# A constant tile multiplied six times a slot in the first batch, and values loaded from SyncE's queue in three portions

## The chip, the cores and the metric

The kernel runs on one core of a Trainium2 chip. A core has TensorE (PE, matmuls; its weight loads are listed apart as PEld), VectorE (DVE), ScalarE (ACT), GpSimd (POOL) and SyncE (SP, which here only issues DMAs). DMAs are issued from SyncE's queue (SPq) or ScalarE's queue (ACTq). The metric is the device time of one execution in microseconds, as the median of the runs.

## The reference

Attention with rotated queries and keys over 4 batches of 8 heads, 576 positions and 64 channels, and then two pairs of dense layers over the 2304 tokens, all in float32:

```python
q_rot, k_rot = (rotate(q), rotate(k))
scores = (1.0 / np.sqrt(D)) * np.matmul(q_rot, k_rot.transpose(0, 1, 3, 2))
scores = scores - np.max(scores, axis=-1, keepdims=True)
attn = np.exp(scores)
attn = attn / (np.sum(attn, axis=-1, keepdims=True) + 1e-09)
x = np.matmul(attn, v)                  # -> x: 2304 tokens of 512 channels
h = x @ w_in;  r = np.maximum(h, 0.0);  x = (s * (r * r) + b) @ w_out
h = x @ w_in2; x = (h / (1.0 + np.exp(-1.702 * h))) @ w_out2
```

## The kernel before, in words

**Slots.** The program is laid out in slots, numbered from below zero up. `at(slot, fn, ...)` puts a task in a slot, and within a slot the table `ORDER` sorts the tasks. Attention takes 144 slots, 36 a batch. A batch has 4 pairs of heads, a pair has two units of 4 and 5 tiles of 128 queries, and each tile is one slot. The tasks of slot n for a tile are: `score_tile` (TensorE writes the scores s of 128 queries against 576 keys into two PSUM banks, of which there is one pair; VectorE reads them into P with the row's minimum, L422; ScalarE takes the exponent, L431), two slots later `turn_tile` (five transposes of P into the PSUM tile t, whose high part ScalarE copies into pt, L491, and whose remainder VectorE takes in every third slot, L497), one slot after that `rest_tile` in the other slots (two matmuls with the constant tile `minus`, then ScalarE, L514), and at the end of a unit `spread_sums` (small matmuls of the row sums with `minus`) and `weighted` (30 matmuls av with the values). TensorE's instructions are chained with `pin` and run in the order in which the code writes them; the other engines' orders come from a scheduler.

**The start.** Before slot 0, `plan_rope` loads the keys and queries of the first pairs (`rope_load`, L257, SyncE's queue), rotates the first pair's on VectorE and the others' on GpSimd (L266 to L274), transposes them on TensorE into r (`rope_turn`, L283), splits r into z (ScalarE's cast of the high part, L295; VectorE's remainder, L296) and places z with DMAs as the operands k and qa of the scores (`place_k`, L321 and L322, four DMAs; `place_qa`, L331 to L333, twelve). A pair's rotated tile is turned in two groups, of 128 and of 64 rows, through a single PSUM bank.

**The values.** `value_load` brings a pair's values with five DMAs (L373 and L378). In the first batch all four pairs are loaded in slot -5, twenty DMAs from ScalarE's queue. `v_top` (slot 1), `v_first` (slot 2) and `v_spread` (slot 3) take the largest magnitude of each head and make its scale, `value_split` (slot 4 for the first pair) splits the values into two float16 parts vz.

**The weights.** In the first batch `weight` loads and converts the first 8 of 16 blocks of the first dense layer pair, in 16 halves: a DMA of 512 KB into a stage tile, then on VectorE L572, L573, L576 and L581 and on ScalarE L571 and L579. These stand from slot 2 on, and the scheduler puts them where it finds room. The dense layers themselves start a few slots after the first batch and then run between the attention of the later batches, by a fixed plan of slots.

## Time and profile before

| what | us |
|---|---|
| median of 3 runs (1296.07 to 1302.21) | 1296.47 |
| the profiled execution's own time | 1298.34 |
| its span, first to last instruction | 1296.6 |
| TensorE busy in the span | 1127.2 |
| VectorE busy | 729.9 |
| ScalarE busy | 676.6 |
| mean granted TensorE clock, share of full | 0.959 |

Times within the profile are microseconds from the span's start. The views used below are: busy time of each engine by stretch ("windows"), instructions in order of time ("timeline", where an entry in brackets is the idle time of the engine just before and what ended it), groups of instructions by line and shape, and DMA issues by line.

### The profile page before, as it was taken

The numbers are of one execution on the slowest core, as the hardware profiler recorded it, in microseconds if no ns is written. First come the engines' busy times: TensorE is split into PE (matmuls) and PEld (weight loads), VectorE is DVE, ScalarE is ACT, GpSimd is POOL, SyncE is SP. The second block draws the span as 40 slices with busy tenths as digits, with TensorE's granted clock in tenths as the row PEclk, the third lists the DMA queues.
The fourth block names the chain that finished last, engine by engine and source line by source line (L and its number), as shares of the span: only waits on it lengthen the run. The fifth ranks groups of instructions, "written<-read, shape, count | busy, mean of one in ns | idle before, by whom it ended". The sixth has DMA issues, their size and how long they took to land.

```text
span 1296.6 us, 20786 instructions
## 1 busy us (share of the span) xinstructions
PE 1127.2 (87%) x7520; PEld 998.5 (77%) x7520; DVE 729.9 (56%) x1653; ACT 676.6 (52%) x1489; POOL 280.4 (22%) x292
## 2 busy tenths in 40 slices
PE   0346777789789899998999999988999999999998
PEld 0235555689689899998999889876888888888887
DVE  5895456879567765666656483667533223232222
ACT  1356665767567666666666575566433223232232
POOL 7631403115414432441111020323000000000000
PEclk9968887899899999999999989999999999999999
DMA  7774576788768776667653384445203012020020
GB/s 205 193 227 101 113 173 208 235 262 260 235 198 238 239 241 179 204 176 213 193 169 120 122 294 132 150 159 177 100 27 104 1 49 82 17 82 16 25 73 17
DMA packets 139398, 194.74 MB, mean 150 GB/s; under 512 B 31648, under 2 KB 103840, under 8 KB 139296
## 3 DMA queue, kind: packets, MB, share of 16 engines
q1 hardware_dynamic: 134368, 192.23, 49.5%
q10 hardware_dynamic: 4928, 1.18, 0.5%
q8 instruction: 60, 0.98, 0.3%
q14 instruction: 42, 0.34, 0.1%
HBM read 145.65 MB, written 40.63 MB: 144 GB/s over the span
## 4 chain that ended last, share of the span: by engine, by line
PE 57%; DMA 10%; issue 8%; DVE 8%; ACT 4%; POOL 1%; SPq 0%; DVEq 0%; ACTq 0%; POOLq 0%
PE acc L99 23%; PE l L99 22%; PE s L99 4%; PE av L99 4%; PE t L99 4%; DMA stage<-in_moe_w_in_dram 3%; DMA stages<-in_moe_w_in_dram 2%; DVE pt L495 1%; DVE P L422 1%; ACT pt L491 1%; DMA qb<-qsp 1%; POOL w L581 1%; ACT P L431 1%; DMA stage<-in_moe_w_out_dram 1%; DMA ksp<-z 1%
## 5 line engine op out<-in xcount | busy, mean ns | idle before, releaser
L99 PE MATMUL l<-xh,w 128*128 128x256 f32 (+1 forms) x1280 | 330.8, 332 | 7.6 <-DVE r L710 4.8
L99 PEld LDWEIGHTS l<-xh,w 128*128 128x128 f32 x1280 | 224.5, 191 | 31.5 <-DVE r L710 8.3
L99 PE MATMUL l<-xl,w 128*128 128x256 f32 (+1 forms) x640 | 211.1, 330 | 0.0
L99 PE MATMUL acc<-w,g 128*128 128x512 f32 x696 | 168.9, 392 | 3.4 <-ACT y L755 3.4
L714 DVE SCALAR_TENSOR_TENSOR r<-r,l 128x256 f32<-128x256 f32 x144 | 60.1, 417 | 180.3 <-ACT r L713 180.3
L442 POOL TENSOR_SCALAR P<-P,st 128x576 f32<-128x576 f32 x108 | 87.7, 812 | 314.8 <-DVE st L441 216.6
L99 PEld LDWEIGHTS acc<-w,g 128*128 128x128 f32 x696 | 131.5, 189 | 31.3 <-ACT y L755 3.8
L431 ACT ACTIVATE P<-P,st 128x576 f32<-128x576 f32 x144 | 111.7, 776 | 75.2 <-DVE P L422 74.7
L713 ACT ACTIVATE r<-l 128x256 f32<-128x256 f32 x144 | 55.1, 382 | 179.0 <-PE l L99 179.0
L422 DVE TENSOR_SCALAR_CACHE_REDUCE P<-s 128x576 f32<-128x576 f32 x144 | 108.5, 754 | 68.0 <-PE s L99 67.1
L99 PEld LDWEIGHTS l<-xl,w 128*128 128x128 f32 x640 | 122.0, 191 | 11.2
L99 PE MATMUL acc<-gh,w 128*128 128x256 f32 x616 | 128.2, 291 | 0.0
L99 PE MATMUL t<-ident,P 128*128 128x128 f32 x720 | 110.1, 287 | 20.7 <-DVE pt L495 9.0
L718 DVE TENSOR_TENSOR g<-r,g 128x256 fp32r<-128x256 f32 x160 | 74.1, 463 | 67.2 <-ACT g L717 67.2
L711 ACT ACTIVATE r<-r,sb 128x256 f32<-128x256 f32 x144 | 86.4, 600 | 49.0 <-DVE r L710 48.8
L491 ACT ACTIVATE pt<-t 128x640 f16<-128x640 f32 x144 | 100.7, 699 | 16.9 <-PE t L99 16.7
L99 PEld LDWEIGHTS t<-ident,P 128*128 128x128 f32 x720 | 86.3, 148 | 28.4 <-issue 19.6
L495 DVE TENSOR_TENSOR pt<-t,pt 128x640 f16<-128x640 f32 x108 | 88.6, 821 | 27.7 <-ACT pt L491 27.4
L99 PEld LDWEIGHTS acc<-gh,w 128*128 128x128 f32 x616 | 103.0, 194 | 0.7 <-DVE part L753 0.2
L717 ACT CAST g<-r 128x256 fp32r<-128x256 f32 x160 | 64.9, 406 | 64.0 <-DVE r L714 63.7
L99 PE MATMUL l<-xh,ws 128*128 128x256 f32 (+1 forms) x384 | 89.4, 311 | 5.3 <-DMA ws<-wd 2.8
L99 PE MATMUL s<-k,qb 128*128 128x320 f32 x480 | 88.1, 311 | 5.0 <-DVE P L422 3.3
(133 smaller groups left out, 2006.4 us busy)
## 6 DMA issues: line engine op xcount, KB each, us to landing
ws<-wd SPq DMA_DIRECT2D x96, 512.0 KB, 4.4
k<-ksp SPq DMA_DIRECT2D x24, 576.0 KB, 5.4
stage<-in_moe_w_in_dram SPq DMA_DIRECT2D x25, 512.0 KB, 4.9
stage<-in_moe_w_out_dram SPq DMA_DIRECT2D x25, 512.0 KB, 4.2
wd<-w SPq DMA_DIRECT2D x14, 512.0 KB, 4.1
xl<-xT SPq DMA_DIRECT2D x11, 512.0 KB, 5.8
xl<-x SPq DMA_DIRECT2D x9, 512.0 KB, 4.3
out_dram<-y SPq DMA_DIRECT2D x36, 128.0 KB, 2.4
```

What stands on the lines that cost most here:

```text
L99: pin(nc.tensor.matmul(*args, **kw))
L422: nc.vector.tensor_scalar(pr, ps[:, 192 : 192 + S], -Q_SCALE, None, op0=ALU.mult, op1=ALU.min, accum_out=st[:, 0:1],)
L431: nc.scalar.activation(pr, pr, AF.Exp, bias=st[:, 0:1], scale=-1.0, accum_out=total)
L442: nc.gpsimd.tensor_scalar(pr, pr, st[:, 2:3], 1.0, op0=ALU.mult, op1=ALU.mult)
L491: nc.scalar.activation(hi, pc, AF.Copy, scale=1.0 if u["b"] else P_SCALE)
L495: nc.vector.tensor_tensor(lo, pc, hi, op=ALU.subtract)
L581: eng.tensor_tensor(lo, f32(low), f32(hi), op=ALU.subtract)
L711: nc.scalar.activation(r, r, AF.Identity, bias=sb[:, 1:2], scale=sb[:, 0:1])
L713: nc.scalar.activation(r, ps[:, cols], AF.Tanh, scale=0.851)
L714: nc.vector.scalar_tensor_tensor(r, r, 1.0, ps[:, cols], op0=ALU.add, op1=ALU.mult)
L717: nc.scalar.copy(gh[:, cols], r)
L718: nc.vector.tensor_tensor(gl[:, cols], r, f32(gh[:, cols]), op=ALU.subtract)
```

## The change

`keep_busy` is new. It multiplies `minus` (128x128, bfloat16) by itself, read twice as 256 columns, and writes columns 768 to 1023 of the current score tile, which nothing reads; it does so three times a call. It is called after the scores of each tile of the first batch, and after each `turn_tile` that falls into a slot of the first batch: 36 and 34 calls, 210 matmuls. `value_load` uses SyncE's queue in the first batch too, in slots -5, -5, -2 and -1 for the four pairs. `v_top`, `v_first`, `v_spread` and the first `value_split` move one slot later.

```diff
+    FILL = 3
+    spare = {}
+    def keep_busy():
+        for _ in range(FILL):
+            mm(spare["s"][:, 768:1024], minus,
+               minus.unsqueeze(1).to_broadcast([128, 2, 128]),
+               start=True, stop=True, skip_group_check=True)
...
-        queue = nc.sync if b else nc.scalar
-        ins = queue.dma_start(vr[64:128, :, 4], vs[:, :, 8])
+        ins = nc.sync.dma_start(vr[64:128, :, 4], vs[:, :, 8])
...
     def score_tile(u):
...
+        if u["b"] == 0:
+            spare["s"] = ps
+            keep_busy()
...
     def turn_tile(u):
...
+        if u["n"] + SKEW_T < bounds[1]:
+            keep_busy()
...
-                at(-5, value_load, b, p, vts[p])
-                at(1, v_top, b, p, vts, first_scale)
-                at(first - 2 if p else 4, value_split, b, p, vts[p])
+                at((-5, -5, -2, -1)[p], value_load, b, p, vts[p])
+                at(2, v_top, b, p, vts, first_scale)
+                at(first - 2 if p else 5, value_split, b, p, vts[p])
...
-    at(2, v_first, 0, first_scale)
-    at(3, v_spread, 0, first_scale)
+    at(3, v_first, 0, first_scale)
+    at(4, v_spread, 0, first_scale)
```

SyncE's queue from its fourth DMA on, before (naturals, nat and values are areas that hold keys and queries as loaded, stage the weights, k00 the first pair's placed keys):

```order
L257 DMA naturals_103<-in_k_dram 128x576 x2
L257 DMA naturals_103<-in_q_dram 128x576 x2
L257 DMA naturals_103<-in_k_dram 128x576
L257 DMA nat020_242<-in_q_dram 128x576
L562 DMA stage0_00_245<-in_moe_w_in_dram 128x4x128
L567 DMA stage0_01_342<-in_moe_w_out_dram 128x512
L562 DMA stage0_10_424<-in_moe_w_in_dram 128x4x128
L567 DMA stage0_11_506<-in_moe_w_out_dram 128x512
L257 DMA nat031_564<-in_k_dram 128x576
L257 DMA values_132<-in_q_dram 128x576
L322 DMA k00_167<-z001_155 64x4x128 x2
```

The same place now (vr00 and vr01 are the first two pairs' values):

```order
L257 DMA naturals_103<-in_k_dram 128x576 x2
L257 DMA naturals_103<-in_q_dram 128x576 x2
L372 DMA vr00_118<-in_v_dram 64x2x64
L372 DMA vr01_125<-in_v_dram 64x2x64
L377 DMA vr00_118<-in_v_dram 64x4x64
L377 DMA vr01_125<-in_v_dram 64x4x64 x2
L377 DMA vr00_118<-in_v_dram 64x4x64
L377 DMA vr01_125<-in_v_dram 64x4x64
L377 DMA vr00_118<-in_v_dram 64x4x64 x2
L377 DMA vr01_125<-in_v_dram 64x4x64
L322 DMA k00_154<-z001_142 64x4x128
L321 DMA k00_154<-z001_142 64x5x128 x2
```

Ten value DMAs have come in ahead of the placing of k00, and two loads of later pairs and all four stage loads have gone behind it: five more value DMAs follow it, then the twelve of qa00, five more of values, and only then the next keys and queries and the first stage. ScalarE's queue, which had the twenty value DMAs ahead of everything, now starts with the first cast of z.

VectorE's order around the first split of z, before (z001 the first pair's keys, vm80 the values' magnitudes):

```order
L274 TENSOR_TENSOR naturals_103<-naturals_103,rot000_113 128x576
L572 TENSOR_SCALAR stage0_00_245<-stage0_00_245 128x512
L572 TENSOR_SCALAR stage0_01_342<-stage0_01_342 128x512
L572 TENSOR_SCALAR stage0_10_424<-stage0_10_424 128x512
L572 TENSOR_SCALAR stage0_11_506<-stage0_11_506 128x512
L296 TENSOR_TENSOR z001_155<-r0010_150,z001_155 128x512
L573 SCALAR_TENSOR_TENSOR stage0_00_245<-stage0_00_245 128x512
L573 SCALAR_TENSOR_TENSOR stage0_01_342<-stage0_01_342 128x512
```

and now (z000 the first pair's queries, P0 to P2 the first three reads of scores; L438 and L590 are the old L422 and L572):

```order
L274 TENSOR_TENSOR naturals_103<-naturals_103,rot000_113 128x576
L296 TENSOR_TENSOR z001_142<-r0010_137,z001_142 128x512
L296 TENSOR_TENSOR z001_142<-r0011_150,z001_142 64x128
L183 TENSOR_REDUCE vm80_246<-vr00_118 128x2
L183 TENSOR_REDUCE vm80_246<-vr01_125 128x2
L296 TENSOR_TENSOR z000_164<-r0000_159,z000_164 128x2x256
L296 TENSOR_TENSOR z000_164<-r0001_174,z000_164 64x2x64
L183 TENSOR_REDUCE vm80_246<-values_167 128x2
L438 TENSOR_SCALAR P0_210,st0_208<-s0_200 128x576
L438 TENSOR_SCALAR P1_222,st1_221<-s1_213 128x576
L183 TENSOR_REDUCE vm80_246<-values_167 128x2
L296 TENSOR_TENSOR z011_231<-r0110_226,z011_231 128x512
```

Before, five of the 16 halves of weights were converted ahead of P0; now none is, and the 16 halves end between P12 and P13 where they ended between P9 and P10. Once the first batch is over TensorE's order is the same in both, and on the other engines rows only change places with their neighbours.

TensorE in slot 2, before (t0 the transposes of P0):

```order
L99 MATMUL s2_233<-k00_167,qa00_184 128x320
L99 MATMUL s2_233<-k00_167,qa01_185 128x320
L99 MATMUL s2_233<-k00_167,qa00_184 128x256
L99 MATMUL s2_233<-k00_167,qa01_185 128x256
L99 MATMUL t0_254<-ident_81,P0_207 128x128 x5
```

and now:

```order
L99 MATMUL s2_234<-k00_154,qa01_179 128x256
L99 LDWEIGHTS minus_90
L99 MATMUL s2_234<-minus_90 128x256
L99 LDWEIGHTS minus_90
L99 MATMUL s2_234<-minus_90 128x256
L99 LDWEIGHTS minus_90
L99 MATMUL s2_234<-minus_90 128x256
L99 MATMUL t0_263<-ident_81,P0_210 128x128 x5
L99 LDWEIGHTS minus_90
L99 MATMUL s2_234<-minus_90 128x256
L99 LDWEIGHTS minus_90
L99 MATMUL s2_234<-minus_90 128x256
```

Three constant matmuls stand behind the scores and three behind the transposes; the first of the latter carries a wait for VectorE, since it writes into a score tile that VectorE reads. Where `spread_sums` follows the transposes, the three stand behind it.

## Rows read from the trace of the kernel before

**Rows 1.** Windows: stretch, length, busy PE PEld DVE ACT POOL, clock, DMA share, GB/s

```profile
0.00:50.66 50.66, 4.71 (x14) 2.74 (x14) 35.87 (x39) 9.05 (x15) 38.37 (x44) 1.00 0.68 168
50.66:56.90 6.24, 4.34 (x19) 3.49 (x19) 3.75 (x8) 2.80 (x6) 1.53 (x2) 1.00 0.95 288
56.90:105.90 49.00, 22.73 (x130) 18.61 (x131) 46.63 (x91) 30.37 (x58) 14.62 (x15) 0.72 0.78 219
105.90:119.02 13.12, 11.06 (x81) 8.54 (x81) 5.49 (x19) 7.84 (x17) 0.00 (x0) 0.74 0.50 96
119.02:206.94 87.92, 63.88 (x505) 51.76 (x504) 42.35 (x118) 54.06 (x115) 26.10 (x27) 0.88 0.60 143
```

**Rows 2.** Timeline of the start: start, duration, engine, line, operation

```profile
0.72 0.74 ACTq L373 DMA_DIRECT2D vr<-in_v_dram  x1
...
9.59 1.09 PE L102 MATMUL r<-ident,naturals 128*128 128x128 f32 x4 [9.59 <-DVE naturals L274]
...
12.12 1.83 DVE L274 TENSOR_TENSOR naturals<-naturals,rot 128x576 f32<-128x576 f32 x1
...
22.35 0.63 ACTq L378 DMA_DIRECT2D vr<-in_v_dram  x1
...
24.30 0.59 ACT L295 CAST z<-r 128x512 fp32r<-128x512 f32 x1
...
24.91 1.44 SPq L322 DMA_DIRECT2D k<-z  x2
24.92 0.69 DVE L296 TENSOR_TENSOR z<-r,z 128x512 fp32r<-128x512 f32 x1 [2.96 <-ACT z L295]
...
27.02 0.26 ACT L295 CAST z<-r 64x128 fp32r<-64x128 f32 x1
...
35.13 0.27 DVE L296 TENSOR_TENSOR z<-r,z 64x128 fp32r<-64x128 f32 x1
...
42.64 0.42 PE L102 MATMUL r<-ident,naturals 128*64 128x128 f32 x1 [6.07 <-DVE z L296]
...
49.08 0.61 SPq L332 DMA_DIRECT2D qa<-z  x1
...
49.56 1.06 PE L99 MATMUL s<-k,qa 128*128 128x320 f32 x3 [3.58 <-DMA qa<-z]
...
50.66 0.76 DVE L422 TENSOR_SCALAR_CACHE_REDUCE P<-s 128x576 f32<-128x576 f32 x1 [0.57 <-PE s L99]
```

**Rows 3.** DMA issues of the first 60 us: KB each, median us to landing

```profile
qa<-z SPq DMA_DIRECT2D x8, 128.0 KB, 2.4
```

**Rows 4.** VectorE's groups from 50.66 to 119.02: busy us, mean ns, idle before

```profile
L581 DVE TENSOR_TENSOR w<-stage,w 128x512 fp32r<-128x512 f32 x11 | 9.3, 845 | 0.6 <-ACT w L579 0.6
L573 DVE SCALAR_TENSOR_TENSOR stage<-stage 128x512 uint32<-128x512 uint32 x11 | 8.6, 789 | 0.7 <-ACT stage L571 0.7
L576 DVE SCALAR_TENSOR_TENSOR stage<-stage 128x512 uint32<-128x512 uint32 x11 | 7.9, 722 | 0.0
L572 DVE TENSOR_SCALAR stage<-stage 128x512 uint32<-128x512 uint32 x11 | 6.7, 613 | 2.0 <-DMA stage<-in_moe_w_in_dram 1.1 <-DMA stage<-in_moe_w_out_dram 0.9
```

**Rows 5.** The same view from 0 to 50.66, one of its groups

```profile
L573 DVE SCALAR_TENSOR_TENSOR stage<-stage 128x512 uint32<-128x512 uint32 x5 | 6.8, 1375 | 0.1
```

**Rows 6.** Timeline of VectorE: the reads P13 and P36

```profile
119.02 0.76 DVE L422 TENSOR_SCALAR_CACHE_REDUCE P<-s 128x576 f32<-128x576 f32 x1 [0.17 <-PE s L99]
...
206.94 0.76 DVE L422 TENSOR_SCALAR_CACHE_REDUCE P<-s 128x576 f32<-128x576 f32 x1 [0.16 <-PE s L99]
```

**Rows 7.** Timeline of TensorE in the first batch

```profile
93.47 2.93 PE L99 MATMUL av<-pt,vz 128*64 128x256 f16 x30
...
124.21 0.42 PE L99 MATMUL t<-minus,rinv 128*64 128x128 bf16 x8 [2.57 <-DVE pt L497]
...
154.17 0.65 PE L99 MATMUL t<-minus,rinv 128*64 128x128 bf16 x8 [3.65 <-DVE pt L497]
```

**Rows 8.** Windows: the last stretch, columns as in rows 1

```profile
900.00:1296.00 396.00, 387.80 (x1792) 323.87 (x1790) 133.09 (x309) 129.42 (x324) 8.24 (x7) 0.99 0.18 54
```

More of the change, by code (lines that the diff above doesn't have):

```diff
@@ L377, in value_load @@
             for h in range(2):
-                queue.dma_start(vr[half * 64 : half * 64 + 64, h, 0:4], vs[:, h, half:8:2])
+                nc.sync.dma_start(vr[half * 64 : half * 64 + 64, h, 0:4], vs[:, h, half:8:2])
         nc.gpsimd.memset(vr[0:64, :, 4, :], 0.0)
@@ L397, in value_split @@
         nc.sync.dma_start(v_spill[b * NP + p], vz.rearrange("p z h c d -> p (z h c d)"))
+    FILL = 3
+    spare = {}
+    def keep_busy():
+        for _ in range(FILL):
+            mm(
+                spare["s"][:, 768:1024],
+                minus,
+                minus.unsqueeze(1).to_broadcast([128, 2, 128]),
+                start=True,
+                stop=True,
+                skip_group_check=True,
+            )
     def score_tile(u):
```

## Prediction

> **What bounds the kernel now.** I read first the windows by stretch, then the start's timeline, then VectorE's groups and TensorE's timeline in the first batch. From 900 us on TensorE is busy 388 of 396 us at nearly its full clock [rows 8]: that part is bound by matmuls, the change leaves it alone, and it starts when the first batch lets it. So the question is when the first batch ends. I mark it by three reads of scores on VectorE: P0 at 50.66 [rows 2], P13 at 119.02 and P36, the first of the second batch, at 206.94 [rows 6].
>
> Up to P0 TensorE works 4.7 of 50.7 us [rows 1]. Its first transposes end at 10.7, but ScalarE issues value DMAs from 0.72 to 22.98 and casts the first z only at 24.30; VectorE then has weights in hand and gives the second, small part of z at 35.13, and the last qa is issued at 49.08 [rows 2]. From P0 to about P10 VectorE is the bound: 46.63 of 49.00 us [rows 1]. From there to P36 no engine is full: TensorE 63.9 of 87.9 us, ScalarE 54.1, VectorE 42.4, at a mean granted clock of 0.88 [rows 1]. Clock levels are two, 2.4 and 1.2 GHz, so 0.88 is about 24% of that stretch, 21 us, at the lower one. After a TensorE gap of 2.57 us eight small matmuls took 0.42 us, after one of 3.65 us the same eight took 0.65 [rows 7].
>
> **Part 1, the start.** ScalarE loses its twenty issues, 0.6 to 0.7 us each and 22.3 us with their waits [rows 2]. The cast of z then waits for TensorE alone. I rebuild the path to P0. VectorE's rotation of keys and queries ends at 12.12 + 1.83 = 13.95 [rows 2]; by then the first group of k is transposed and cast. Its remainder takes 0.69, then the second group needs TensorE 0.42, ScalarE 0.26 and VectorE 0.27 [rows 2]: 15.6. SyncE's ten value issues ahead of the placing go out while the rotation runs. One of the four k DMAs can go before 15.6, three follow at 0.72: 17.8. Then five value issues at 0.63: 20.9; twelve of qa at 0.61: 28.2; 2.4 to landing [rows 3]: 30.6; the last three score matmuls 1.06 [rows 2]: 31.7. P0 is read at about **32**, 18.7 us earlier. The transposes of q fall inside this, between 15.6 and 20.9.
>
> The upper bound for P0 comes from ScalarE's pace with waits, 22.3/20 = 1.1 us an issue. Ten from about 6 us would then end at 17, the four of k at 20, five values at 25.5, qa, landing and matmuls as above: P0 at 36.4. The Trainium skill, "DMA: Bandwidth & Descriptors", section "Issuing engines are not separate DMA queues", says that issuing from a second engine saves only the sequencer's time for issuing. By it the change gives that saving away, which speaks for the bound of 36.4; the trace shows the issue times, 0.61 to 0.74 us, but not how much of them hides.
>
> **Part 2, VectorE from P0 to P13.** This is where most of the head start is paid back. Five of 16 halves of weights used to be converted before P0, at VectorE's leisure; now none, and all 16 must be done before P13. From P0 to P13 VectorE was busy 3.75 + 46.63 + 5.49 = 55.9 of 68.4 us [rows 1]. Added are five halves. At this stretch's means a half costs 0.845 + 0.789 + 0.722 + 0.613 = 2.97 us [rows 4], five 14.8, and one value reduction of 0.8 moves too: 71.5 us. VectorE's densest stretch ran at 46.63/49.00 = 95% [rows 1], so 75.3 us: P13 at 32 + 75.3 = 107.3, a gain of **11.7**. Bounds: if the five halves fit into the 12.5 us in which VectorE was idle there, the whole 18.7 stays. If they cost what they cost beside a busy GpSimd at the start (L573 1375 ns against 789 here, 1.74 times [rows 4, 5]), they are 25.9, the sum 82.6, at 95% 87 us: P13 at 119, gain 0. GpSimd was busy 38.4 of the first 50.7 us [rows 1], and its later pairs' rotation also moves behind P0, since their loads stand behind the values; hence not the low price. I take the mean of this stretch, the nearest row.
>
> **Part 3, the constant matmuls.** Eight of 128 columns took 0.42 us at the full clock [rows 7], so one of 256 columns costs 0.105 us and six a slot 0.63. Up to P13 TensorE waits for VectorE and they cost nothing, save through the wait on VectorE that the three behind the transposes carry: the rotated groups' transposes and the 30 matmuls av stand behind it. At most two av groups of 2.93 us [rows 7] come late, at least none; I take 1 us. From P13 to P36 there are 23 slots, 138 matmuls, 14.5 us. TensorE was idle 24.0 us there [rows 1], chiefly at the ends of units, where it has run ahead and waits for the copies of t, 2.57 and 3.65 us in the two rows shown [rows 7]. A matmul ahead of such a gap shortens it, one behind it does not. I let 60% hide: cost **6**; bounds 0 and 14.5.
>
> **Part 4, the clock.** Of the 21 us at 1.2 GHz TensorE is busy some 15 (63.9/87.9), and at 2.4 GHz the same work takes 0.42/0.65 of it: 5.4 us less; the bound is half, 7.7. I take **5**, the clock nearly restored; the lower bound is 0. If it stays restored the gaps decide what is late next: the copies on ScalarE.
>
> The Trainium skill, "TensorE: Matmul & The Clock Gate", section "Why this matters for your kernels", says that idle gaps between bursts are what drops the clock. The trace agrees, 0.42 us after the short gap and 0.65 after the long one. By that rule the matmuls behind `spread_sums` come after the gap and cannot prevent the drop; it is the third rival.
>
> **Part 5, the rest.** `v_top` to `value_split` one slot later costs nothing: the first av comes two slots behind `value_split`. After P36 the orders agree, so the shift passes on.
>
> **Sum**: 11.7 - 1 - 6 + 5 = 9.7 us. The profiled execution, 1298.34 with a span of 1296.6, would become 1288.6. It lies 1.9 above the median of the runs, which I forecast: 1296.47 - 9.7 = **1287**.
>
> **Rivals.** First, more comes through: GpSimd disturbs the moved conversions little, so P13 gains 15, the constant matmuls hide in the 24 us and the clock gives 6: 21 us, 1275. For it: VectorE's idle 12.5 us and TensorE's 24. Against: 95% busy where the halves must go. Chance 0.17.
>
> Second, VectorE takes the head start back, at the start's prices: P13 gains 0 to 4, the rest is even: 1292 to 1297. For it: the start's price [rows 5], and the first stage loads now leave SyncE only after the last values, past 30 us, while VectorE's queue is strict, so that a late stage holds the P behind it. Chance 0.22.
>
> Third, slower: the clock is not restored, because the gaps at unit ends stay, and the 138 matmuls stand on TensorE's path at 14.5 us, of which 24% at 0.65/0.42 add 1.9. With 11.7 - 1 from the start the sum is +5.7, 1302; with P13 gaining only 5, 1309. It decides the sign from the point where the unhidden part exceeds the gain at P13. Against: 24 us of idle TensorE. Chance 0.10, nearly all slower than 0.5%.
>
> Fourth, the move of the queue doesn't free the start as it says: SyncE becomes the queue that everything waits in. P0 at 36.4, 4.4 of the gain gone: 1291. Chance 0.09.
>
> **How the numbers follow.** The forecast, 1280 to 1290, has 0.42. Faster or slower by 0.5% is 6.5 us, about what a measurement of this kernel can tell from no change: below 1290 or above 1303. Faster: 0.42 + 0.17 = 0.59. Same: 0.22 + 0.09 + 0.01 = 0.32. Slower: 0.09. The range takes the first rival's 1275 and a little below, the second's and fourth's whole, and the third's start: 1273 to 1300.
>
> **What would show it.** P0 between 30 and 36 us and ScalarE's first cast before 14 (part 1). VectorE over 90% busy from about 40 us to P13, P13 near 107 (part 2); near 100 the first rival, near 118 the second. From P13 to P36 some 87 us with a clock near 1.0 (parts 3 and 4); a clock still under 0.9 and over 92 us is the third rival. Matmuls of `minus` at 0.1 us each. It is wrong if P13 comes before 98 or after 118, or if the stretch behind P36 changes its length by more than 3 us.

## Result and the profile after

The changed kernel takes **1307.0 us** (median of 6 runs, 1299.1 to 1312.2), the kernel before beside it 1299.7 (median of 6): 1.0056 times, 95% interval 1.0032 to 1.0080, so 4 to 10 us slower. The forecast was 1287 with a range of 1273 to 1300, and 0.59 for faster. The profiled execution took 1308.29 us, its span is 1306.5.

Windows of the changed kernel, columns as in [rows 1], cut at its own P0, P13 and P36:

```profile
0.00:29.47 29.47, 5.34 (x17) 3.06 (x17) 10.08 (x18) 2.97 (x5) 11.39 (x24) 1.00 0.63 143
29.47:117.59 88.12, 47.95 (x300) 36.44 (x301) 79.04 (x136) 47.09 (x91) 44.23 (x37) 0.75 0.77 213
117.59:208.02 90.43, 74.05 (x640) 58.91 (x639) 42.31 (x118) 54.16 (x114) 26.61 (x27) 0.98 0.56 132
...
900.00:1296.00 396.00, 391.27 (x1800) 326.62 (x1799) 137.94 (x316) 132.08 (x330) 10.84 (x8) 0.99 0.18 55
```

P0 is at 29.47 instead of 50.66, 21.2 us earlier. P13 is at 117.59 instead of 119.02 [rows 6]: 19.8 of these 21.2 us are gone. P36 comes at 208.02 instead of 206.94. From P0 to P13 VectorE is busy 79.0 of 88.1 us, GpSimd 44.2, where GpSimd had 38.4 us of its work before P0 [rows 1]. From P13 to P36 the clock is 0.98 instead of 0.88, and yet the stretch is 2.5 us longer than before.

Timeline of the start after, as in [rows 2]:

```profile
0.73 1.28 ACT L295 ACT_TABLE_LOAD   x1 [0.73 <-PEq L1095]
...
4.02 1.51 SPq L372 DMA_DIRECT2D vr<-in_v_dram  x2
5.58 6.58 SPq L377 DMA_DIRECT2D vr<-in_v_dram  x8
...
11.68 0.59 ACT L295 CAST z<-r 128x512 fp32r<-128x512 f32 x1 [9.67 <-PE r L102]
...
12.29 0.63 SPq L322 DMA_DIRECT2D k<-z  x1
...
26.48 0.60 SPq L333 DMA_DIRECT2D qa<-z  x1
...
29.47 0.76 DVE L438 TENSOR_SCALAR_CACHE_REDUCE P<-s 128x576 f32<-128x576 f32 x1 [7.45 <-PE s L99]
...
31.55 0.43 SPq L580 DMA_DIRECT2D stage<-in_moe_w_in_dram  x1
```

The first cast of z is at 11.68 instead of 24.30, the last qa at 26.48 instead of 49.08. The first load of weights leaves at 31.55, after P0. So VectorE, busy 35.9 us before P0 in the kernel before, is busy 10.1 us before it now, and idle 19.4.

VectorE's groups of the conversion from P0 to P13, as in [rows 4]:

```profile
L591 DVE SCALAR_TENSOR_TENSOR stage<-stage 128x512 uint32<-128x512 uint32 x16 | 15.6, 978 | 0.1
L594 DVE SCALAR_TENSOR_TENSOR stage<-stage 128x512 uint32<-128x512 uint32 x16 | 14.8, 928 | 0.0
L599 DVE TENSOR_TENSOR w<-stage,w 128x512 fp32r<-128x512 f32 x16 | 12.9, 811 | 0.0
L590 DVE TENSOR_SCALAR stage<-stage 128x512 uint32<-128x512 uint32 x16 | 10.4, 651 | 4.5 <-DMA stage<-in_moe_w_out_dram 3.1 <-DMA stage<-in_moe_w_in_dram 1.4
```

All 16 halves stand behind P0, at 3.37 us the half (the four means together) where the prediction took 2.97. The timeline of VectorE and GpSimd around the reads P4 (51.65) and P5, and then around P7 (88.14), shows where the difference comes from:

```profile
49.78 1.36 DVE L462 TENSOR_SCALAR sums<-sums 128x4 f32<-128x4 f32 x1
51.05 0.68 DVE L594 SCALAR_TENSOR_TENSOR stage<-stage 128x512 uint32<-128x512 uint32 x1
51.07 1.92 POOL L274 TENSOR_TENSOR nat<-nat,rot 128x576 f32<-128x576 f32 x1
...
62.06 1.85 POOL L271 TENSOR_TENSOR naturals<-naturals,tab 128x576 f32<-128x576 f32 x1
62.56 1.69 DVE L389 SCALAR_TENSOR_TENSOR vz<-vr,vsc,vz 128x320 f16<-128x320 f32 x1
...
63.87 3.45 POOL L274 TENSOR_TENSOR naturals<-naturals,rot 128x576 f32<-128x576 f32 x2
64.18 1.88 DVE L594 SCALAR_TENSOR_TENSOR stage<-stage 128x512 uint32<-128x512 uint32 x1
65.98 2.69 DVE L389 SCALAR_TENSOR_TENSOR vz<-vr,vsc,vz 128x320 f16<-128x320 f32 x2
68.70 0.76 DVE L438 TENSOR_SCALAR_CACHE_REDUCE P<-s 128x576 f32<-128x576 f32 x1
...
84.76 0.68 DVE L599 TENSOR_TENSOR w<-stage,w 128x512 fp32r<-128x512 f32 x1
...
85.12 1.58 POOL L274 TENSOR_TENSOR naturals<-naturals,rot 128x576 f32<-128x576 f32 x1
85.36 1.89 DVE L591 SCALAR_TENSOR_TENSOR stage<-stage 128x512 uint32<-128x512 uint32 x1
...
88.81 0.69 DVE L594 SCALAR_TENSOR_TENSOR stage<-stage 128x512 uint32<-128x512 uint32 x1
...
89.42 0.69 DVE L591 SCALAR_TENSOR_TENSOR stage<-stage 128x512 uint32<-128x512 uint32 x1
```

GpSimd rotates almost without a pause from 33.7 to 76.0, so at 51.05 as well as at 64.18: beside it the step L594 took 0.68 us once and 1.88 another time. The clean pair is around P7, where a single step of GpSimd's rotation stands, at 85.12: L591 beside it took 1.89 us, L591 at 89.42, with GpSimd idle, 0.69. So it is in the whole trace: of the conversion's steps that the timeline lists one by one, the 33 with GpSimd idle took 0.42 to 0.69 us (mean 0.61), the 20 wholly beside it 0.41 to 1.89 (mean 1.18). DMA traffic does not go with it; here is the stretch of the rotation, and then one with GpSimd idle:

```profile
33.70:76.00 42.30, 14.90 (x79) 10.85 (x77) 39.71 (x55) 18.71 (x37) 41.73 (x31) 0.64 0.77 213
93.80:117.20 23.40, 16.33 (x133) 12.92 (x132) 20.36 (x49) 17.09 (x36) 0.00 (x0) 0.93 0.82 228
```

DMA is as busy in the second (0.82) as in the first (0.77), and no step there took over 0.69 us. At 0.61 us the 64 steps of the 16 halves would take 39 us; they took 53.7. P5 is read at 68.70, 17 us behind P4, after the conversions and the splits of values that stand ahead of it.

### The profile page after: what moved, and what is told of

It is laid out like the page before. It is cut to its first block, busy times and chain, and to the rows that moved or that the text cites. A ratio compares the mean times of both kernels' runs of the same rounds, so it can differ in the third digit from the quotient of the medians.

```text
span 1306.5 us, 21190 instructions
## 1 busy us (share of the span) xinstructions
PE 1155.1 (88%) x7730; PEld 1017.2 (78%) x7730; DVE 728.3 (56%) x1653; ACT 676.8 (52%) x1489; POOL 280.2 (21%) x292
## 4 chain that ended last, share of the span: by engine, by line
PE 56%; DMA 10%; DVE 8%; issue 8%; ACT 2%; SPq 1%; POOL 1%; DVEq 0%; POOLq 0%; ACTq 0%
PE acc L99 23%; PE l L99 22%; PE s L99 4%; PE av L99 4%; PE t L99 3%; DMA stage<-in_moe_w_in_dram 3%; DMA stages<-in_moe_w_in_dram 2%; DMA ws<-wd 1%; DVE pt L511 1%; DVE P L438 1%; DMA x<-y 1%; POOL w L599 1%; DMA vr<-in_v_dram 1%; DVE stage L594 1%; DMA qb<-qsp 1%
## 5 line engine op out<-in xcount | busy, mean ns | idle before, releaser
L458 POOL TENSOR_SCALAR P<-P,st 128x576 f32<-128x576 f32 x108 | 88.1, 816 | 323.9 <-DVE st L457 216.7
L438 DVE TENSOR_SCALAR_CACHE_REDUCE P<-s 128x576 f32<-128x576 f32 x144 | 108.5, 754 | 68.0 <-PE s L99 66.2
L99 PE MATMUL l<-xh,ws 128*128 128x256 f32 (+1 forms) x384 | 90.3, 313 | 7.2 <-DVE r L728 4.3
```

Of the source, the lines that this page charges most:

```text
L99: pin(nc.tensor.matmul(*args, **kw))
L438: nc.vector.tensor_scalar(pr, ps[:, 192 : 192 + S], -Q_SCALE, None, op0=ALU.mult, op1=ALU.min, accum_out=st[:, 0:1],)
L458: nc.gpsimd.tensor_scalar(pr, pr, st[:, 2:3], 1.0, op0=ALU.mult, op1=ALU.mult)
```

## Experiments

All kernels of a group ran on one chip, beside the kernel before. Ratios are to it, with 95% intervals; one per cent is 13 us. P0, P13, P36, P50 are reads of scores in the profiled execution of each kernel; "P50 on" is from P50 to the last read, P143. The ratio is of medians, the reads are of one execution each, and that one can lie some us off its kernel's median: 8.0 us below it in e5, 6.8 above it in e9.

| kernel | ratio | P0 | P13 | P36 | P13-P36 | P36-P50 | P50 on |
|---|---|---|---|---|---|---|---|
| before | 1 | 50.66 | 119.02 | 206.94 | 87.9 | 64.7 | 454.6 |
| before, again (e15) | 0.9987 (0.9961-1.0014) | 50.51 | 115.30 | 202.44 | 87.1 | 65.0 | 454.5 |
| changed | 1.0056 (1.0032-1.0080) | 29.47 | 117.59 | 208.02 | 90.4 | 64.6 | 460.3 |
| changed, again (e1) | 1.0072 (1.0048-1.0095) | 29.73 | 119.57 | 209.85 | 90.3 | 67.3 | 459.3 |
| loads only (e2) | 1.0058 (1.0041-1.0075) | 28.97 | 117.41 | 204.52 | 87.1 | 69.1 | 457.6 |
| constants only (e3) | 1.0096 (1.0076-1.0116) | 51.02 | 123.76 | 213.93 | 90.2 | 68.7 | 457.6 |
| loads, constants behind scores (e8) | 0.9975 (0.9950-1.0000) | 30.21 | 113.10 | 201.71 | 88.6 | 63.7 | 459.4 |
| before, less conversion (e5) | 0.9911 (0.9881-0.9940) | 50.97 | 103.08 | 191.40 | 88.3 | 66.8 | 452.7 |
| loads, less conversion (e7) | 0.9830 (0.9805-0.9855) | 28.77 | 90.54 | 186.68 | 96.1 | 63.1 | 458.6 |
| e8 + early keys, queries (e9) | 1.0020 (1.0002-1.0037) | 32.09 | 117.68 | 208.13 | 90.5 | 65.8 | 459.2 |
| e9 + four early halves (e10) | 0.9990 (0.9969-1.0011) | 43.06 | 117.57 | 205.09 | 87.5 | 63.3 | 453.2 |
| changed, order back (e11) | 1.0049 (1.0030-1.0068) | 29.45 | 119.90 | 210.63 | 90.7 | 63.5 | 458.0 |
| before, order swapped (e12) | 1.0008 (0.9989-1.0026) | 50.78 | 115.04 | 203.80 | 88.8 | 65.3 | 457.9 |
| e8, paced (e13) | **0.9891** (0.9867-0.9915) | 29.42 | 96.25 | 191.14 | 94.9 | 63.5 | 454.2 |
| before, paced slower (e14) | 0.9993 (0.9976-1.0010) | 38.53 | 91.52 | 196.15 | 104.6 | 70.8 | 458.6 |
| loads, paced (e16) | 0.9963 (0.9937-0.9988) | 28.85 | 102.65 | 200.54 | 97.9 | 67.3 | 457.2 |
| changed, paced (e17) | 1.0018 (0.9991-1.0045) | 29.44 | 101.87 | 201.28 | 99.4 | 67.7 | 457.5 |
| before, paced (e18) | 0.9914 (0.9889-0.9939) | 38.22 | 96.30 | 195.66 | 99.4 | 64.5 | 455.1 |

### Which part of the change costs

Theory 1 was the prediction's second rival: VectorE takes the head start back. Theory 2: the constant matmuls eat it.

The changed kernel once more:

> The changed kernel a second time. What is open is the part of its trace behind P36, where the read of P number 80 stood level with the kernel before and number 140 stood 6.7 us later, though the instructions are the same there. If this late loss is chance (a clock that happened to fall at a gap), the second trace has P116 to P140 within 3 us of P80's shift, and the median over rounds comes to within 3 us of the kernel before, some 1300 to 1302. If it follows from the change, P140 is again 5 us or more behind its place before, and the median is again 6 to 8 us above the kernel before.

Measured: 1306.78 (before 1297.23). The late loss is there again, in part: P36 is 2.9 us behind the first trace of the kernel before, P140 10.2. So it is not the chance of one execution.

The loads moved, no constant matmuls:

```
-    FILL = 3
+    FILL = 0
```

> The value loads moved as in the change, no constant matmuls (FILL = 0). Theory 1, VectorE takes the head start back by itself: P0 near 29.5, P13 at 114 to 119 as in the changed kernel (117.6) or little before, mean granted clock from P13 to P36 again near 0.88, the time within 4 us of the kernel before. Theory 2, the constant matmuls behind the transposes hold TensorE until VectorE has read the last scores and so eat the head start: without them P13 comes at 107 to 111 and P36 at 196 to 199, the time 7 to 10 us under the kernel before.

Measured: 1304.22. P0 21.7 us early, P13 only 1.6: the head start is lost without any constant matmul. Theory 1 holds for it up to P36, theory 2's numbers fail; theory 1's time, within 4 us of the kernel before, fails too, at 7.0 above. Behind P36, which is 2.4 us early, it loses another 7 in the profiled execution, which neither theory named.

Constant matmuls on the kernel before, whose loads of values and slots stay as they were (the edit against it, without `keep_busy` itself):

```
+        if u["b"] == 0:
+            spare["s"] = ps
+            keep_busy()
...
+        if u["n"] + SKEW_T < bounds[1]:
+            keep_busy()
```

> The constant matmuls as in the change, the value loads as before (ScalarE's queue, slot -5). Theory 1: the first stretch is bound by VectorE with or without them, P0 and P13 where they were, 50.7 and 119 to 120; the stretch P13 to P36 runs at a clock near 0.98 and takes 88 to 91 us as in the changed kernel (90.4, against 87.9 before); the time is 0 to 4 us above the kernel before. Theory 2: they cost the 8 to 10 us that the prediction had missing, P13 at 126 or later, the time 8 us or more above the kernel before.

Measured: 1308.82, 11.6 above; P13 at 123.76, P36 at 213.93. The clock from P13 to P36 is 0.98, and it does not pay. Between the two theories: the constants cost 5 to 9 us by P13 even where TensorE waits for VectorE anyway.

Only those behind the scores:

```
-        if u["n"] + SKEW_T < bounds[1]:
-            keep_busy()
```

> The changed kernel without the three constant matmuls behind the transposes; the three behind the scores stay, which wait for nothing that TensorE had not waited for already. Theory 1: P13 at 114 to 119 still, the time within 3 us of the changed kernel, and perhaps a lower clock from P13 to P36, 0.90 to 0.95. Theory 2: the waits of these matmuls for VectorE's read (6.0 us at 44.3, 3.1 us from P13 to P36) were the loss: P13 at 107 to 111 and the time 6 us or more under the changed kernel.

Measured: 1294.88, 11.9 us below the changed kernel on the same chip. So both theories hold for a part each: the head start is still mostly lost (P13 at 113.10), and the three constants behind each `turn_tile` cost 8 to 12 us (3.6 of the 11.9 lie from P36 to P50, where no constant stands). The waits of TensorE from P0 to P13 say how (engine, line, what it waited for: total, times, longest); first the changed kernel, with the row of its timeline where the longest of them stands, then the kernel without them:

```profile
PE s L99 <- DVE P L438: 17.0, 8, 6.0
```

```profile
44.33 0.80 PE L99 MATMUL s<-minus 128*128 128x256 bf16 x3 [6.00 <-DVE P L438]
```

```profile
PE s L99 <- DVE P L438: 11.1, 4, 7.9
```

These matmuls write into the score tile that VectorE has not read yet, so TensorE stands at them, with the transposes of the next pair behind them, for as long as VectorE's order puts conversions ahead of that read. The rows show where TensorE stands, not that this wait is the whole price: other waits shrink, and its idle time from P0 to P13 is 40.2 us with these matmuls and 38.3 without. Those behind the scores follow matmuls that had waited for the same tile already.

### What takes the head start back

The two steps L573 and L576 left out of the early conversions, in the kernel before and in the one with the loads moved:

```
+        if late or f >= SPLIT:
+            nc.vector.scalar_tensor_tensor(
+                low, high, 0x80000000, low, op0=ALU.bitwise_and, op1=ALU.bitwise_or
+            )
+            nc.vector.scalar_tensor_tensor(
+                low, high, 3, low, op0=ALU.logical_shift_left, op1=ALU.bitwise_or
+            )
```

> The kernel before with two of VectorE's four steps of the weights' conversion (L573 and L576) left out for the first 8 blocks in the first batch, so that the weights of these blocks are not the reference's. It is the base for the next kernel. Eleven or twelve of the 16 halves are converted behind P0, at 0.79 + 0.72 us the half: P13 17 us or so earlier than in the kernel before, at 100 to 106, if VectorE is the bound there; at 114 or later if it is not.

> The moved value loads without constant matmuls, and the same two conversion steps left out (weights of the first 8 blocks not the reference's). Theory 1, VectorE's work behind P0 (16 halves of weights, beside GpSimd's rotation) takes the head start back: with half of that work gone, more of the 21 us survives to P13 than the 1.6 us that survived with all of it; P13 stands 8 us or more ahead of that of the kernel before with the same steps left out. Rival: the head start is lost to something else that every variant has (the values' scale chain, TensorE's order, the placing of later pairs on SyncE's queue): the lead at P13 stays at 0 to 4 us.

Measured: 1290.42 and 1278.38. P13 at 103.08 and at 90.54: with half of the conversion gone, 12.5 us of the head start reach P13 where 1.6 did, and the moved loads gain 12 us where with all of it they lose 7. Windows from P0 to P13 of the two, first the kernel before:

```profile
50.97:103.08 52.11, 36.16 (x228) 29.44 (x229) 33.10 (x86) 36.12 (x75) 13.98 (x16) 0.80 0.84 226
```

```profile
28.77:90.54 61.77, 36.19 (x228) 28.14 (x229) 52.98 (x97) 42.39 (x85) 40.32 (x36) 0.78 0.90 251
```

In the two traces 4.7 of the 12.5 us are left at P36: from P13 on TensorE is busy 70.0 us in the second kernel and 64.2 in the first, at a granted clock of 0.82 against 0.88. How much of that the medians share is open, since the first kernel's profiled execution is its fastest, 1282.46 us, and the second's took 1280.93.

To give VectorE its early work back: keys and queries of pairs 1 and 2 from ScalarE's queue, so that GpSimd rotates earlier, and in a second kernel four loads of weights as well. Both start from e8:

```
+        queue = nc.scalar if b == 0 and p in (1, 2) else nc.sync
+        queue.dma_start(
...
+        early = nc.scalar if not late and f < 2 else nc.sync
...
+            early.dma_start(raw, w_out[f * 128 : (f + 1) * 128, :])
```

> The value loads moved and the three constant matmuls behind the scores kept, those behind the transposes left out (as in the kernel whose P13 stood 5.9 us early); in addition the keys and queries of pairs 1 and 2 are loaded from ScalarE's queue, which is free up to its first cast at 12, so that GpSimd rotates them before P0 as it did in the kernel before. Theory 1 with the price on GpSimd (VectorE's steps take 1.9 us instead of 0.7 beside it): GpSimd busy 25 us or less from P0 to P13 instead of 48, VectorE's busy time there 6 us or more below 75.3, P13 at 100 to 107. Rival, the number of conversion steps alone is the price: P13 stays at 111 to 115.

> As the kernel with the early keys and queries, and the first four stage loads of weights from ScalarE's queue too, so that VectorE converts four halves before P0, as the kernel before did with five. Theory 1: four halves at 3 us less behind P0, but the casts of z stand behind four stage copies on ScalarE, P0 some 3 to 8 us later than 30; VectorE busy from P0 to P13 some 12 us less than without; P13 at 95 to 103, the time 5 us or more under that of the kernel with the early keys and queries alone. Rival: P0 slips by as much as the four halves are worth, and P13 stays where it was.

Both missed: 1301.28 and 1298.98, P13 at 117.68 and 117.57. Windows of the first, then of the second, up to P0 and from there to P13:

```profile
0.00:32.09 32.09, 5.35 (x17) 3.07 (x17) 9.99 (x17) 2.97 (x5) 19.79 (x32) 1.00 0.62 149
32.09:117.68 85.59, 44.54 (x267) 34.83 (x268) 76.11 (x136) 47.66 (x91) 34.02 (x28) 0.72 0.75 213
```

```profile
0.00:43.06 43.06, 5.38 (x17) 3.07 (x17) 29.40 (x33) 7.77 (x13) 24.59 (x32) 1.00 0.63 160
43.06:117.57 74.51, 43.83 (x267) 35.08 (x268) 63.92 (x120) 42.49 (x83) 34.21 (x28) 0.75 0.79 211
```

GpSimd works 34.0 us beside VectorE instead of the 48.1 of e8 (25 or less were expected), and VectorE's work is not less (76.1 against 75.3): of the conversion's steps 17 instead of 26 stand wholly beside GpSimd, but they take 1.21 us on average instead of 1.03. That steps beside GpSimd are slow is seen in the rows; that moving its rotation would give the time back is not shown. In the second kernel P0 slips by about what the four halves are worth and P13 stays, as its rival said. The sum is what counts. Up to P13 VectorE works 35.9 + 55.9 = 91.7 us and idles 27.3 in the kernel before; 10.1 + 79.0 = 89.1 and 28.5 in the changed one; 93.3 and 24.2 in the last. The wait for the values' loads had been VectorE's time for weights; shorter, it held no weights.

### The order behind P36

The prediction said that the orders agree behind P36, and the section on the change that other engines' rows only change places with their neighbours. VectorE's order is a scheduler's, and it differs up to P50. The difference in the kernels above: in the kernel before, VectorE's read r of the second block of the dense layers stands ahead of the split xl of the second pass's input (1.2 us), in the changed one behind it. Timeline of VectorE and TensorE there, before and after:

```profile
242.06 0.41 DVE L710 TENSOR_TENSOR r<-r,l 128x256 f32<-128x256 f32 x1
...
242.53 0.39 PE L99 MATMUL l<-xh,ws 128*128 128x256 f32 x1 [1.58 <-DVE r L710]
...
243.06 1.21 DVE L674 TENSOR_TENSOR xl<-xl,xh 128x1024 fp32r<-128x1024 f32 x1
```

```profile
243.48 1.22 DVE L692 TENSOR_TENSOR xl<-xl,xh 128x1024 fp32r<-128x1024 f32 x1
...
244.68 0.41 DVE L728 TENSOR_TENSOR r<-r,l 128x256 f32<-128x256 f32 x1
...
245.14 0.39 PE L99 MATMUL l<-xh,ws 128*128 128x256 f32 x1 [3.48 <-DVE r L728]
```

One order is put back in the changed kernel (xl made to stand behind r; the edit is shown), and the other forced on the kernel before (the same edit with the two instructions exchanged):

```
+            if n == 1 and i == 0:
+                tc.add_manual_dep(
+                    ins.ins,
+                    held[0].name,
...
+                if n == 0 and f == 1:
+                    held.append(ins.ins)
```

> The changed kernel with one order put back: VectorE's split of the second pass's x (L692, xl, 1.2 us) stands again behind the read r of the second block of the first pass (L728), as in the kernel before, instead of ahead of it. Theory, this order costs: in all six traces with xl ahead the matmuls l wait 2.9 to 3.5 us for r behind the 44th read of scores and the slot from P43 to P44 takes 7.3 to 11.4 us, in the four with r ahead 1.6 and 6.4. So here a wait of about 1.6 us, a slot of 6.4 to 7, and P50 minus P36 some 2 to 4 us less than in the changed kernel; the median 1302 to 1305 where the changed kernel has 1307. Rival, the late loss has another cause and the order is only its companion: the slot stays above 9 us, or the time comes out where it was, 1306 to 1308.

> The kernel before with the opposite order forced: r of the second block (L710) behind the split xl of the second pass (L674). Theory, this order costs: the wait of l for r 2.9 to 3.5 us instead of 1.6, the slot from P43 to P44 9 to 11 us instead of 6.4, the time 2 to 4 us above the kernel before. Rival: the slot grows, but the next slots give it back, as the changed kernel's did between P44 and P47, and the time stays within 1 us.

Measured: 1303.25 and 1300.39, 1.0049 and 1.0008. In the first the slot from P43 to P44 takes 7.0 us instead of 9.8 and 11.4, the wait is 2.30, P36 to P50 63.5 instead of 64.6 and 67.3. In the second the slot takes 9.35, the wait is 3.42, and P36 to P50 65.3 instead of 64.7 and 65.0. So this one order lengthens its slot by some 3 us. By P50 that is worth 1.1 and 3.8 us in the changed kernel, and only about 0.5 in the kernel before, where the next slots give it back as the rival said; the intervals of the ratios overlap those of their bases, so no time is shown for it. The orders as a whole go with more: the seven traces where the scheduler put r first took 64.0 us from P36 to P50 on average (63.1 to 65.0), the seven where it put it second 67.6 (64.6 to 70.8). That r and xl alone don't make this is seen in e16 and e17 below, where r was put first in an otherwise other order, and the stretch took 67.3 and 67.7.

### Conversions behind the reads

No conversion is needed before the second batch, and VectorE is busy only 42 of 88 us from P13 to P36 [rows 1]. So in these kernels VectorE's first step of half j has to stand behind the read P of slot 1.5 j (in the slower one of slot 2 + 2 j); nine or six halves are begun ahead of P13 instead of 16:

```
+    def paced(ins, f, m):
+        n = int(1.5 * (2 * f + m))
+        if not late and f < SPLIT and 0 <= n:
+            tc.add_manual_dep(
+                ins.ins,
+                reads[min(n, len(reads) - 1)],
...
-        nc.vector.tensor_scalar(low, low, 29, None, op0=ALU.logical_shift_right)
+        paced(nc.vector.tensor_scalar(low, low, 29, None, op0=ALU.logical_shift_right), f, m)
```

> The moved value loads, constant matmuls behind the scores only, and the 16 weight halves spread: VectorE's first step of half j stands behind the read P of slot 1.5 j, so that the last comes at P23 instead of P13. Theory 1, the conversions stand in front of the reads of scores and take the head start back, and nothing needs them before the second batch: VectorE 55 to 62 us busy from P0 to P13, P13 at 95 to 103, and P36 at 190 to 197; the time 1283 to 1291. Rival, seen in the kernel with half of the conversions left out, where 12 us of lead at P13 shrank to 5 at P36: another bound between P13 and P36 takes it back, P13 under 105 but P36 at 199 or later, the time 1292 or more.

> The kernel before with the halves spread (half j behind the read P of slot 2 + 2 j), loads of values as before. Theory 1: VectorE is the bound from P0 to P13 here too, though the five halves that filled its wait before P0 now come behind it; 28 of 64 steps or so remain ahead of P13: P13 at 105 to 111, P36 at 196 to 201, the time 5 to 9 us under the kernel before. That would say that most of what is to be had lies in the order of the conversions and not in the move of the loads. Rival: P13 stays at 115 or later, because TensorE waits for something else, and the time within 3 us.

Measured: 1284.02 and 1297.23 (before 1298.81). The first is faster than the kernel before by 14 us (11 to 17), and than the changed kernel by more. Its windows from P0 to P13 and on to P36:

```profile
29.42:96.25 66.83, 41.69 (x267) 33.74 (x268) 57.44 (x109) 38.77 (x78) 45.69 (x36) 0.80 0.79 212
96.25:191.14 94.89, 68.19 (x574) 55.28 (x572) 61.65 (x147) 61.56 (x128) 26.52 (x27) 0.95 0.69 177
```

All of theory 1's numbers for it came in. VectorE's work is spread, 57.4 us from P0 to P13 and 61.7 behind it; against e8 the stretch ahead of P13 shrinks by 16 us (82.9 to 66.8) and the one behind grows by 6. The second kernel missed its forecast of the time (5 to 9 us less): P13 came at 91.52, far ahead of the 105 expected, but the last halves stand behind slot 32, P13 to P36 takes 104.6, and P36 to P50 70.8 with r second in the order. P13 as the mark was not enough.

Last, what is left of each part of the change under this pace, and how far two executions of one kernel differ:

> The kernel before, a second trace. Chance theory: P13 between 114 and 120 and the stretch from P50 to the last read of scores (454.6 us in the first trace, 457.9 in a kernel with the same instructions there) some 3 us longer this time. Rival: P13 within 0.5 us of 119.0 and that stretch within 0.5 us of 454.6, so that the changed kernel's 459.3 to 460.3 are its own.

> The moved value loads, conversions spread (half j behind P of slot 1.5 j), no constant matmuls, and the split of the second pass's x kept behind the read of the second block, so that the order there is that of the kernel before. Theory, the constant matmuls behind the scores bring little: P13 within 2 us of 96.3, the mean clock from P13 to P36 near 0.85 instead of 0.95, P36 at 190 to 194 and the time 1283 to 1288 (with them 1284). Rival, they bring the clock and with it time: P36 at 195 or later and 1288 or more.

> The changed kernel, all its constant matmuls included, with the conversions spread (half j behind P of slot 1.5 j) and the order of the second pass's split kept. Theory, those behind the transposes cost time by themselves (their wait for VectorE's read, and 0.5 us a slot on TensorE): P13 at 98 to 102, the stretch P13 to P36 2 us or more longer than the 94.9 with those behind the scores alone, P36 4 to 7 us later than 191.1, the time 1288 to 1291. Rival, they only cost where VectorE is the bound: P36 within 2 us of 191 and the time 1283 to 1286.

> The kernel before with conversions spread in the same way (half j behind P of slot 1.5 j) and nothing else. It is the base for what the moved loads are worth. In the kernel with the slower pace P0 came at 38.5, since VectorE no longer had weights in hand before the first split of z; so P0 near 39 here too, 9 to 10 us behind that with the moved loads. If that difference passes on to P36 once the conversions stand behind the reads: P36 at 198 to 202, the time 1291 to 1294. If the later bounds take it back: P36 at 191 to 195 and 1284 to 1288.

Measured: 1298.98, 1295.73, 1300.91 and 1289.27 (before 1300.18).

The kernel before again: P13 is 3.7 us and P36 4.5 us earlier than in its first trace, but the stretch from P50 on is the same to 0.1 us. The chance theory was right on P13, the rival on that stretch.

The pace alone (e18) is worth 11 us. It also brings P0 to 38.2, since VectorE no longer has weights in hand before the first split of z. Moved loads on top, without constants (e16), lose: P0 9.4 us earlier, P13 6.4 later (e16 also holds xl behind r, which acts behind P36). Windows from P0 to P13, first the kernel before paced, then with the loads moved:

```profile
38.22:96.30 58.08, 37.17 (x228) 30.94 (x229) 47.91 (x106) 36.38 (x74) 18.07 (x18) 0.82 0.66 177
```

```profile
28.85:102.65 73.80, 39.36 (x228) 31.04 (x229) 60.59 (x107) 39.99 (x79) 41.66 (x36) 0.68 0.77 199
```

GpSimd works 42 us beside VectorE instead of 18, and VectorE is busy 60.6 us instead of 47.9 with 107 instructions against 106, the same nine halves among them. The granted clock is 0.68 instead of 0.82, but TensorE's work grows by only 2.2 us with it. I had expected the constants behind the scores to bring little there; 9 us lie between e16 and e13 at P36, and 9 by the ratios (measured on two chips, and e13 without the held order).

With all constants (e17) P36 is at 201.28, 10 us behind e13, and the time of 1300.91 lies above the 1288 to 1291 expected: those behind the transposes cost also where the conversions are spread. From P13 to P36 TensorE is busy 77.2 us instead of 68.2, at the same clock of 0.95:

```profile
101.87:201.28 99.41, 77.18 (x640) 60.96 (x639) 60.51 (x147) 61.22 (x126) 28.00 (x27) 0.95 0.64 161
```

Whether moved loads with constants behind the scores (e13, 0.9891) beat the pace alone (e18, 0.9914) is not settled: the intervals overlap.

## Why the prediction was wrong

**Part 1** was right. P0 came at 29.47, 2.5 us ahead of the forecast and just outside the 30 to 36 named, the first cast at 11.68. The Trainium skill, "DMA: Bandwidth & Descriptors", section "Issuing engines are not separate DMA queues", says that issuing from several engines saves only the time of issuing; the prediction took this as speaking for its bound of 36.4. The trace shows P0 7 us ahead of that bound: the ten value loads ahead of the placing were out at 12.16, half a us after the first cast of z began.

**Part 2 failed**, at the price of the halves of weights. The forecast from P0 to P13 was 71.5 us of VectorE's work at 95%, P13 at 107.3; it became 79.0 at 90%, P13 at 117.6 to 119.9 in three executions with the change. The price per half was 3.37 us, not 2.97: 16 times 0.40 are 6.4 of the 7.5 us too few. Another 4.5 us VectorE waited for stage loads that leave SyncE's queue only at 31.55. I had both ends on paper, a gain of 0 at the start's price, and took the mean of a stretch in which GpSimd worked 16 us, though the prediction itself said that its rotation moves into the stretch; it worked 44 there. The start's price had been weighed for five halves only, while any of the 16 could stand beside the rotation. The second rival, at 0.22, had place and mechanism right (P13 "near 118"), though not its end: it let the rest come out even.

That the conversions behind P0 take the head start back is shown: it is lost without any constant matmul (e2), 12.5 us of it reach P13 with half of the conversion left out (e5, e7), and with the conversions spread P13 comes at 96.25 with the constants behind the scores (e13) and at 102.65 with none (e16).

For the slowed steps the Trainium skill, "SBUF — State Buffer", section "Who interferes with whom", says that VectorE and GpSimd share a pair of ports under an exclusive lock. The rows agree (0.69 us for L591 with GpSimd idle, 1.89 beside its rotation); the kernel that moved 14 us of rotation away showed no less work on VectorE, so no run here shows that the rule sets the time.

Three traces of the changed start with all constants have P13 at 119.02 on average. Three traces of the start before (two executions, and e12 with the same instructions up to there) have it at 116.45 on average, and vary from 115.0 to 119.0. So **P13 is 2.6 us later**, not 10.7 earlier; the spread leaves open whether it is later or even. This step is 13 us of the error.

**Parts 3 and 4** came near in their sum, in part by luck. From P13 to P36 they forecast +1 us, 6 for the constants less 5 for the clock. Measured were +2.5 (90.5 against 87.9, three traces each), and the clock went to 0.98, as forecast, so the third rival's "not restored" was wrong. For the whole, +2 was forecast; with the loads moved, all the constants cost 2.6 us at the medians of one chip (1304.22 to 1306.78, with intervals that overlap). But that is the difference of two larger effects that the prediction did not have: the constants behind the transposes cost 8 to 12 us (e8 against the changed kernel), those behind the scores gain some 10 (e8 against e2), of which 5 lie from P36 to P50 in the scheduler's order. On the kernel before both together cost 11.6. I had seen that those behind the transposes wait for VectorE's read, and gave that 1 us; up to P13 TensorE waited 17.0 us for such reads with them and 11.1 without.

The Trainium skill, "TensorE: Matmul & The Clock Gate", section "Why this matters for your kernels", advises to avoid idle gaps between bursts of matmuls, since they drop the clock. The trace agrees as to the clock, 0.98 instead of 0.88 with 16 instead of 24 us of idle TensorE; the time did not fall with it.

**Part 5 failed.** "After P36 the orders agree" is true of TensorE, not of VectorE, whose scheduled order differs up to P50; the one pair that was swapped made 0.5 to 4 us there. The prediction's own sign of being wrong, more than 3 us behind P36, came true: from P36 to the end the changed kernel's first trace takes 1098.5 us and that of the kernel before 1089.7. From P50 on VectorE's order agrees too, and still the changed start's three traces take 458.0 to 460.3 us up to P143, the kernel before 454.6 and 454.5, and e12 with the same instructions 457.9. That is 3.5 us more on average, with other kernels between 452.7 and 459.4, and another 2.1 us come behind P143. Windows from P50 to P143, before and after:

```profile
271.66:726.25 454.59, 419.73 (x3664) 403.18 (x3663) 299.75 (x753) 291.87 (x639) 140.75 (x155) 0.98 0.67 204
272.65:732.99 460.34, 425.41 (x3664) 407.98 (x3663) 301.71 (x752) 291.71 (x639) 138.62 (x155) 0.97 0.66 201
```

So nearly all of the 5.7 us between these two are longer work of TensorE on the same 3664 matmuls, at a slightly lower clock; over the three traces of each it is 2.4 of the 3.5. What lowers the clock there stays open.

By these traces the steps add up to 2.6 + 2.5 + 5.8 (behind P36: 0.2 up to P50, 3.5 up to P143, 2.1 after) = 10.9 us slower; measured were 7.3 and 9.6 us at the medians.

## What to carry to other kernels

A wait that an engine fills with work it has to do anyway is not idle time: count the bound engine's work and its idle time up to the mark, and ask which of the two the change makes smaller. Work that is due much later but ready early is best held behind the reads that others wait for; that was worth 11 us here (e18), where the earlier start by itself cost 7 (e2). And where a scheduler sets an engine's order, look for the end of the reordering on every engine: an edit in one batch moved the next.

## What the runs showed of the hardware

- In the changed kernel's trace a conversion step of VectorE on 128x512 took at most 0.69 us with GpSimd idle, and up to 1.89 beside GpSimd's rotation, though not always: 20 such steps took 0.41 to 1.89, 1.18 on average. Tiny steps were hit as hard: 1.36 us for 128x4 beside the rotation, where 0.17 was usual.
- Two executions of one kernel, 1298.34 and 1293.6 us, differ by 3.7 us at P13 with the same instructions; one trace of each kernel cannot tell less than that.
- With an earlier start TensorE's granted clock from P0 to P13 was lower: 0.68 instead of 0.82 of full speed, where 39 us of work were spread over 74 us instead of 37 over 58 (e16 and e18).
